# Top-k attention with an MLP behind it: scores in quarters of the PE array, and the left-over keys of the values in quarters too

## The chip, the core and the metric

The kernel runs on one core of a Trainium2 chip. The metric is the device time of one execution in microseconds, the median of several runs. Below, PE is TensorE (with its queue of stationary loads, PEld), DVE is VectorE, ACT is ScalarE, POOL is GpSimd and SP is SyncE, which issues the DMAs.

## The reference

Attention of 8 batches with 8 heads, 576 rows and 64 dimensions a head, in which each row keeps its 32 largest scores; behind it an MLP with a leaky ReLU over 4608 tokens of 512 features. All of it is in 32-bit floating point.

```python
scores = scale * np.matmul(q, k.transpose(0, 1, 3, 2))
kth = np.partition(scores, -32, axis=-1)[..., -32:-31]
scores = np.where(scores >= kth, scores, -1000000000.0)
attn = np.exp(scores - np.max(scores, axis=-1, keepdims=True))
attn = attn / (np.sum(attn, axis=-1, keepdims=True) + 1e-09)
x = np.matmul(attn, v)          # then (B, S, H*D), as 4608 x 512
h = x @ w_in                    # 512 x 2048
out = np.maximum(0.01 * h, h) @ w_out
```

## The kernel before, in words

**Units.** The 64 heads are held as 32 pairs, four pairs to a batch; a pair has the 64 dimensions of head 0 on partitions 0 to 63 and those of head 1 on 64 to 127. A unit is 128 rows of scores for each of two heads. 576 rows are four times 128 and 64 left over, so there are two sorts: a whole unit has 128 rows of one pair, and a grouped unit has the 64 left-over rows of two pairs, that is of four heads. A batch has 16 whole and 2 grouped units, 144 units in all. In batches 0, 2, ... the grouped units come last, in 1, 3, ... first (L202 to L206). Two neighbours in this order, here called a couple, always belong to the same sort, and for whole units to neighbouring pairs.

**Steps.** The loop at L609 has a step s for every unit. In a step DVE finds the top 32 of unit s (`top_k`, L289); POOL masks unit s-1 and ACT takes its exponents; unit s-2 is normalized by ACT, split into its 16-bit halves (L339), written to DRAM and read back transposed (L344), which gives `wT`, the weights by key. Work is issued in an order written out by hand, and each engine goes through its own queue in that order.

**Scores** (`scores`, L208) are made in even steps for a couple two units ahead. The 576 keys are cut into 352 and 224. A unit's 352 keys go to a PSUM tile "wide" of two banks (two such tiles rotate), and the 224 keys of both units share one tile "narrow". A head has its own bank (index i at L225). For a whole unit a matmul has 64 dimensions on one half of the rows of the array and 128 columns (rows of scores): two for each part, head 0 on the upper rows and head 1 on the lower. For a grouped unit a matmul has 64 rows and 64 columns, four for each part. ACT copies the results to `s_sb` (L232).

**Values** (`weigh_values`, L374; called by `values`, L593) are made for a couple as soon as its weights are there: in the middle of a step for units 0 to 13, at the end of a step afterwards (`values_at`, L495). Keys are taken in five chunks. Four are of 128 keys. The fifth holds the 64 left-over keys of both heads: the weights of head 0 on partitions 0 to 63, those of head 1 on 64 to 127 (`vk` has zeros in the half that belongs to the other head). A matmul has the 128 keys on the rows of the array and the 64 value dimensions on half of its columns; head 0 and head 1 take the two halves in turn. Each unit of a couple takes 10 matmuls with 128 columns moving; a grouped one takes 20 with 64 moving. All go to one bank of a "wide" tile, and ACT copies them to x (`keep_values`, L388, L395), where x tile number p holds the two heads of pair p on its 128 partitions.

**Order of the two.** Up to step 19 (`HURRY` = 20) the scores stand ahead of the values at the end of a step, afterwards the values stand ahead of the scores (L663 to L667). Three couples (`HURRIED`) have their values in an odd step, where no scores are made. For 12 units the scores are made at the start and kept in DRAM (`keep_scores`, `fetch_scores`), so six even steps make none.

**MLP** (`mlp`, L425). Chunks of 256 tokens (the first two 128) go through `w_in` (L437) and `w_out` (L449) in small portions between the attention work; `slot_budget` and `mlp_cost` decide from counts of columns how many portions stand in each slot. They know nothing of the cost of scores and values. What is left over at the end runs in one stretch. An f32 matmul shows in the trace as two records, each with its own stationary load.

Of the kernel before, what the change touches and what calls it, by code (L numbers as in the profile page):

```python
# [9 lines left out]
F32 = mybir.dt.float32  # L10
# [6 lines left out]
NKC = 5  # L17
# [3 lines left out]
def kernel(  # L21
# [13 lines left out]
    nc = tc.nc  # L35
    NPAIR, P, S = qT.shape
    D = P // 2
# [7 lines left out]
    HP = DMODEL // P  # L45
# [6 lines left out]
    LEFT = S % P  # L52
# [14 lines left out]
    ps_sc = ctx.enter_context(tc.tile_pool(name="ps_sc", bufs=1, space=bass.MemoryType.PSUM))  # L67
# [13 lines left out]
    w_in = [const.tile([P, DFF], F32, name=f"w_in{c}") for c in range(HP)]  # L81
# [78 lines left out]
    qk_of, v_of = {}, {}  # L160
# [20 lines left out]
    class Unit:  # L181
# [3 lines left out]
        def __init__(self, b, pairs, q0):  # L185
# [10 lines left out]
                self.outs = [(pairs[0], 0, LEFT), (pairs[1], LEFT, 0)]  # L196
            self.pairs = pairs

    units = []
    for b in range(B):  # L200
        first = b % 2 == 1
# [6 lines left out]
    def scores(us):  # L208


        narrow = ps_sc.tile([P, 2, 512], F32, name="narrow")
        ps = {}
        for k, u in enumerate(us):
            wide = ps_sc.tile([P, 2, 512], F32, name="wide", bufs=2)
            ps[u] = ((wide[:, :, 0:WIDE], 0, WIDE),
                     (narrow[:, :, k * NARROW:(k + 1) * NARROW], WIDE, S))

        order = ((us[0], 0), (us[0], 1), (us[1], 1), (us[1], 0))
        for u, part in order:
            to, k0, k1 = ps[u][part]  # L220
            for n in range(0, len(u.parts), 2):
                for i, pi, side, r0 in u.parts[n:n + 2]:
                    qt, kt = qk_of[pi]
                    d = slice(side * D, (side + 1) * D)
                    nc.tensor.matmul(to[r0:r0 + u.rows, i, :], qt[d, u.q0:u.q0 + u.rows],  # L225
                                     kt[d, k0:k1], start=True, stop=True)
        for u in us:
            u.both = work.tile([P, 2, S], F32, name="s_sb", bufs=5)
            u.s = [u.both[:, i, :] for i in range(2)]
        for u, part in order:  # L230
            to, k0, k1 = ps[u][part]
            nc.scalar.copy(u.both[:, :, k0:k1], to)  # L232
# [131 lines left out]
    x_of = {}  # L364

    def x_at(token):

        c = 0
        while token >= CHUNKS[c]:
            token -= CHUNKS[c]  # L370
            c += 1
        return c, token

    def weigh_values(u, po):  # L374
        n = u.rows
        po = po.rearrange("p (o n) -> p o n", n=n)
        for o, (pi, r0, r1) in enumerate(u.outs):
            vt = v_of[pi]
            for c in range(NKC):
                for side, r in ((0, r0), (1, r1)):  # L380
                    nc.tensor.matmul(  # L381
                        po[side * D:(side + 1) * D, o, :],
                        vt[:, c, side, :],
                        u.wT[:, c + side * NKC if c + 1 < NKC else c, r:r + n],
                        start=(c == 0), stop=(c == NKC - 1),
                    )

    def keep_values(u, po):  # L388
        n = u.rows
        po = po.rearrange("p (o n) -> p o n", n=n)  # L390
        ch, col = x_at(u.b * S + u.q0)
        if ch not in x_of:
            x_of[ch] = [xpool.tile([P, CHMAX], F32, name=f"x{c}") for c in range(HP)]
        for o, (pi, _, _) in enumerate(u.outs):
            nc.scalar.copy(x_of[ch][pi % HP][:, col:col + n], po[:, o, :])  # L395

    EARLY = 2

# [90 lines left out]
    HURRY = 20  # L489
# [3 lines left out]
    MIDDLE, END = 0, 1  # L493

    def values_at(n):  # L495

        if n < UNHURRIED:
            return (n | 1) + LAG + 1, MIDDLE
        return (n | 1) + LAG - ((n | 1) in HURRIED), END
# [10 lines left out]
    for n, u in enumerate(steps):  # L510
        ch, _ = x_at(u.b * S + u.q0)
# [5 lines left out]
    def attended(*place):  # L517
        for at, ch in ready_at:
            if at == place:
                ready.append(ch)  # L520
                backlog[0] += mlp_cost(ch)
# [12 lines left out]
    with tc.manual_schedule():  # L534
# [57 lines left out]

        def values(*place):  # L593
            due = [u for n, u in enumerate(steps) if values_at(n) == place]
            if due:
                po = ps_sc.tile([P, 2, 512], F32, name="wide", bufs=2)[:, 0, 0:2 * P]
                po = po.rearrange("p (u n) -> p u n", u=2)
            else:
                return ()
            for n, u in enumerate(due):  # L600
                weigh_values(u, po[:, n, :])
            return [(u, po[:, n, :]) for n, u in enumerate(due)]

        def keep(weighed, *place):
            for u, po in weighed:
                keep_values(u, po)
            attended(*place)

        for s in range(len(steps) + LAG + 1):  # L609
# [18 lines left out]
            if older and not late and not at_first:  # L628
                weights_of(older)
            mlp_steps(budget)  # L630
            weighed = values(s, MIDDLE)
            at_once = s - 2 in HASTY or any(at == (s, MIDDLE) for at, _ in ready_at)
            if at_once:
                keep(weighed, s, MIDDLE)
# [24 lines left out]
            if not at_once:  # L659
                keep(weighed, s, MIDDLE)  # L660
            if new and new[0] in early_units:
                new = ()
            if new and s < HURRY:  # L663
                scores(new)
            keep(values(s, END), s, END)
            if new and s >= HURRY:
                scores(new)  # L667
# [63 lines left out]
```

## Time and profile before

| what | us |
|---|---|
| median of 3 runs | 1464.25 (1464.2 to 1464.74) |
| the profiled execution | 1463.63 |
| its span, first to last instruction | 1461.7 |
| PE busy in it | 1405.5 |
| second layer of the MLP, L449, 1152 records of 128x512 | 505.1 |
| first layer of the MLP, L437, 2176 records of 128x256 | 482.6 |
| values, L381, 3200 records | 179.0 |
| scores, L225, wide tiles of whole units, 280 + 176 records of 64x352 | 60.1 + 35.0 |
| scores, L225, narrow tiles of whole units, 280 + 176 records of 64x224 | 34.9 + 21.3 |
| copies of values to x, L395, 160 | 32.2 |

Busy times of rows overlap where matmuls run beside each other. In a row of the profile, "128*64" is the part of the array that a record uses, rows by columns; "128x128" behind it is the moving operand, partitions by columns. The interval from one start to the next measures a stage better than the duration of a record, since the end of a matmul is modelled.

### The profile page before, as it was taken

To read this page: it belongs to the slowest core of one execution; us is meant where nothing else is said; L and a number is where in the kernel's file an instruction comes from. 1 tells how busy PE (TensorE), PEld (TensorE's weight loads), DVE (VectorE), ACT (ScalarE), POOL (GpSimd) and SP (SyncE) were. 2 spreads that over 40 slices of the span, in tenths; PEclk is the share of its full clock that TensorE was granted. 3 is DMA by queue.
4 is the path that set the end of the run, shared out by engine and by line. 5 is a ranking of instruction groups with operands and counts; after the bars stand their busy time and mean duration, and the time that the engine had idled before them with its cause. 6 is when DMAs were issued, how large, how long until landed. Compare 5 with 4: busy or idle time off the path is not lost.

```text
span 1461.7 us, 24213 instructions
## 1 busy us (share of the span) xinstructions
PE 1405.5 (96%) x8066; PEld 932.9 (64%) x8068; DVE 1320.3 (90%) x3401; ACT 1100.9 (75%) x1984; POOL 1097.8 (75%) x744
## 2 busy tenths in 40 slices
PE   7848999999989999999999999999999999999998
PEld 2425548576757676767676767676766666666674
DVE  7999999999999999999999999999999999999600
ACT  8878878677868777777778787777777777777710
POOL 3288888878888888888888787888887878787700
PEclk9968999999999999999999999999999999999999
DMA  8967543646576666676656655666566665554510
GB/s 320 344 219 225 140 119 101 194 128 181 151 192 179 172 167 188 156 194 169 157 163 170 169 138 141 171 164 166 149 156 171 164 151 143 153 141 130 150 43 14
DMA packets 394989, 239.03 MB, mean 164 GB/s; under 512 B 334576, under 2 KB 336112, under 8 KB 392944
## 3 DMA queue, kind: packets, MB, share of 16 engines
q1 hardware_dynamic: 394864, 237.48, 58.5%
q8 instruction: 63, 1.03, 0.3%
q14 instruction: 62, 0.51, 0.1%
HBM read 55.77 MB, written 99.09 MB: 106 GB/s over the span
## 4 chain that ended last, share of the span: by engine, by line
PE 77%; DVE 13%; ACT 4%; DMA 4%; issue 1%; SPq 0%; POOL 0%; DVEq 0%; ACTq 0%; POOLq 0%
PE pz L449 30%; PE ph L437 29%; PE wide L381 10%; DVE tops L301 5%; PE wide L225 5%; DVE pairs L304 4%; PE narrow L225 3%; DMA apart<-split 2%; ACT split L339 1%; DVE pairs L296 1%; DMA raw<-in_weights_dram 1%; ACT s_sb L318 1%; ACT s_sb L330 1%; DVE w_out L156 1%; DMA wT<-apart 1%
## 5 line engine op out<-in xcount | busy, mean ns | idle before, releaser
L314 POOL TENSOR_SCALAR pen<-s_sb,tops 128x576 f32<-128x576 f32 x288 | 638.3, 2216 | 203.8 <-DVE tops L301 135.6
L301 DVE MAX8 tops<-pairs 128x8 f32<-128x288 f32 (+1 forms) x1152 | 635.9, 591 | 0.0
L449 PE MATMUL pz<-w_out,gT 128*128 128x512 f32 x1152 | 505.1, 595 | 2.4 <-ACT scale L410 2.4
L437 PE MATMUL ph<-x,w_in 128*128 128x256 f32 x2176 | 482.6, 381 | 0.0
L304 DVE MATCH_REPLACE8 pairs<-tops,pairs 128x288 f32<-128x288 f32 (+1 forms) x864 | 460.1, 538 | 0.0
L437 PEld LDWEIGHTS ph<-x,w_in 128*128 128x128 f32 x2176 | 409.5, 190 | 75.5 <-issue 21.3
L315 POOL TENSOR_TENSOR s_sb<-s_sb,pen 128x576 f32<-128x576 f32 x288 | 406.9, 1413 | 24.0
L449 PEld LDWEIGHTS pz<-w_out,gT 128*128 128x128 f32 x1152 | 216.4, 190 | 266.2 <-issue 261.2
L339 ACT COPY split<-s_sb 128x1152 uint16<-128x1152 uint16 x280 | 309.5, 1146 | 1.7 <-DMA apart<-split 1.7
L330 ACT ACTIVATE s_sb<-s_sb,rz 128x576 f32<-128x576 f32 x288 | 207.7, 773 | 33.4 <-DVE rz L327 33.4
L318 ACT ACTIVATE s_sb<-s_sb,nbias 128x576 f32<-128x576 f32 x288 | 222.4, 772 | 6.4 <-POOL s_sb L315 6.4
L296 DVE TENSOR_TENSOR pairs<-s_sb 128x576 f32<-128x576 f32 x288 | 213.6, 780 | 9.5
L381 PEld LDWEIGHTS wide<-wT,vt 128*64 128x64 f32 x3200 | 161.2, 139 | 53.0 <-issue 36.2
L381 PE MATMUL wide<-wT,vt 128*64 128x128 f32 (+1 forms) x3200 | 179.0, 268 | 10.3 <-DMA wT<-apart 4.7
L443 ACT ACTIVATE gT<-ph 128x512 f32<-128x512 f32 x136 | 80.7, 593 | 58.6 <-PE ph L437 57.7
L395 ACT COPY x<-wide 128x128 f32<-128x128 f32 (+1 forms) x160 | 32.2, 260 | 120.2 <-PE wide L381 120.2
L232 ACT COPY s_sb<-wide 128x704 f32<-128x704 f32 x130 | 98.0, 754 | 20.1 <-PE wide L225 20.1
L458 ACT COPY o_sb<-pz 128x512 f32<-128x512 f32 x36 | 21.1, 585 | 92.3 <-PE pz L449 92.2
L225 PE MATMUL wide<-kt,qt 64*128 64x352 f32 (+1 forms) x360 | 70.4, 507 | 1.0 <-ACT s_sb L247 0.7
L232 ACT COPY s_sb<-narrow 128x448 f32<-128x448 f32 x130 | 62.9, 536 | 1.2 <-PE narrow L225 0.6
L304 DVE MATCH_VALUE_LOAD pairs<-tops,pairs 128x8 f32 x864 | 62.6, 72 | 0.0
L327 DVE RECIPROCAL rz<-ze 128x2 f32<-128x2 f32 x144 | 22.3, 155 | 42.3 <-ACT ze L323 42.1
(67 smaller groups left out, 678.0 us busy)
## 6 DMA issues: line engine op xcount, KB each, us to landing
apart<-split SPq DMA_DIRECT2D x280, 288.0 KB, 2.1
raw<-in_weights_dram SPq DMA_DIRECT2D x15, 1024.0 KB, 6.9
vt<-in_vk_dram SPq DMA_DIRECT2D x32, 320.0 KB, 3.7
out_dram<-o_sb SPq DMA_DIRECT2D x36, 256.0 KB, 2.8
kept<-gT SPq DMA_DIRECT2D x12, 576.0 KB, 3.2
s_sb<-kept SPq DMA_DIRECT2D x12, 576.0 KB, 4.8
qt<-in_qT_dram SPq DMA_DIRECT2D x20, 288.0 KB, 3.5
kt<-in_kT_dram SPq DMA_DIRECT2D x20, 288.0 KB, 3.4
```

What stands on the lines that cost most here:

```text
L225: nc.tensor.matmul(to[r0:r0 + u.rows, i, :], qt[d, u.q0:u.q0 + u.rows], kt[d, k0:k1], start=True, stop=True)
L296: nc.vector.tensor_tensor(pairs[:, :, n, :], u.both[:, :, 0:HS], u.both[:, :, HS:S], op)
L301: nc.vector.max(out=u.tops[:, i, r, :], in_=rest[i])
L304: nc.vector.match_replace(out=rest[i], in_to_replace=u.tops[:, i, r, :], in_values=rest[i], imm_value=LOWEST)
L314: nc.gpsimd.tensor_scalar(pen, u.s[i], u.tops[:, i, ROUNDS - 1, 7:8], MASKED, ALU.is_lt, ALU.mult)
L315: nc.gpsimd.tensor_tensor(u.s[i], u.s[i], pen, ALU.add)
L318: nc.scalar.activation(u.s[i], u.s[i], AF.Exp, bias=u.nbias[:, i:i + 1], scale=SCALE, accum_out=u.z[:, i:i + 1])
L330: nc.scalar.activation(u.s[i], u.s[i], AF.Copy, bias=0.0, scale=u.rz[:, i:i + 1])
L339: nc.scalar.copy(split, pairs[:, :, h])
L381: nc.tensor.matmul(po[side * D:(side + 1) * D, o, :], vt[:, c, side, :], u.wT[:, c + side * NKC if c + 1 < NKC else c, r:r + n], start=(c ...
L437: nc.tensor.matmul(ph[:, i, 0:n], w_in[c][:, f * P:(f + 1) * P], x[c][:, 0:n], start=(c == 0), stop=(c == HP - 1),)
L449: nc.tensor.matmul(pz[0:m, 0:DMODEL], gT[:, f, r0:r0 + m], w_out[f // 4][:, f % 4, :], start=(f == 0), stop=(f == NFC - 1),)
```

## The change

**Scores.** A whole unit's matmuls are cut into rows 0 to 63 and 64 to 127: four of 64 x 64 for each part where there were two of 64 x 128. A grouped unit's are the same as before, in the same order.

**Values of whole units** (`weigh_whole`). A couple is done together. The two halves of columns now belong to the two units, the two banks of the "wide" tile to the two heads. Four chunks of keys are as before but for the order. The fifth is taken in 64-row pieces: only the head's own 64 keys, so that the four matmuls of a chunk (two heads by two units) lie on the four quarters of the array. These stand last where the scores follow (from step 20), first otherwise; for units 0 to 13 the fifth chunk stays 128 rows with its zeros.

**Values of grouped units** (`weigh_left`) take the same matmuls with halves of columns by pair and banks by head.

**x** now has head 0 of two neighbouring pairs in one tile, head 1 in the next; the host puts the rows of `w_in` in the same order.

```diff
+            self.quarters = [(i, pi, side, r0 + r, q0 + r) for r in range(0, self.rows, LEFT)
+                             for i, pi, side, r0 in self.parts]
...
-            for n in range(0, len(u.parts), 2):
-                for i, pi, side, r0 in u.parts[n:n + 2]:
+            for n in range(0, len(u.quarters), 4):
+                for i, pi, side, r0, q0 in u.quarters[n:n + 4]:
                     qt, kt = qk_of[pi]
                     d = slice(side * D, (side + 1) * D)
-                    nc.tensor.matmul(to[r0:r0 + u.rows, i, :], qt[d, u.q0:u.q0 + u.rows],
+                    nc.tensor.matmul(to[r0:r0 + LEFT, i, :], qt[d, q0:q0 + LEFT],
                                      kt[d, k0:k1], start=True, stop=True)
...
-    def weigh_values(u, po):
...
+    def weigh_whole(us, po, order):
+        for m, c in enumerate(order):
+            for side in range(2):
+                k = slice(side * LEFT, (side + 1) * LEFT) if c == QUARTERS else slice(0, P)
+                at = min(c, NKC - 1)
+                for n, u in enumerate(us):
                     nc.tensor.matmul(
+                        po[n * D:(n + 1) * D, side, 0:P],
+                        v_of[u.pairs[0]][k, at, side, :],
+                        u.wT[k, at + side * NKC if at + 1 < NKC else at, :],
+                        start=(m == 0), stop=(m == NKC - 1),
+                    )
+
+    def weigh_left(u, po):
+        for c in range(NKC):
+            for side in range(2):
+                for o, (pi, *rows) in enumerate(u.outs):
+                    r = rows[side]
+                    nc.tensor.matmul(
+                        po[o * D:(o + 1) * D, side, :],
+                        v_of[pi][:, c, side, :],
+                        u.wT[:, c + side * NKC if c + 1 < NKC else c, r:r + LEFT],
                         start=(c == 0), stop=(c == NKC - 1),
                     )
...
+    def keep_values(pair, po, b, q0):
+        ch, col = x_at(b * S + q0)
...
+        for side in range(2):
+            nc.scalar.copy(x_of[ch][pair % HP + side][:, col:col + po.shape[-1]], po[:, side, :])
+
+    QUARTERS = NKC
+    FULL = list(range(NKC - 1))
...
+            po = ps_sc.tile([P, 2, 512], F32, name="wide", bufs=2)
+            if len(due[0].pairs) == 1:
+                weigh_whole(due, po, FULL + [NKC - 1] if place[1] == MIDDLE else
+                            [QUARTERS] + FULL if place[0] < HURRY else FULL + [QUARTERS])
+                return [(due[0], po[:, :, 0:P])]
             for n, u in enumerate(due):
+                weigh_left(u, po[:, :, n * LEFT:(n + 1) * LEFT])
+            return [(u, po[:, :, n * LEFT:(n + 1) * LEFT]) for n, u in enumerate(due)]
...
+        w_in = w_in.reshape(2, 2, 2, 64, 2048).transpose(0, 2, 1, 3, 4)
```

## The prediction, made before the change was run

> **What bounds the kernel now.** I read the page first: busy shares, the slices, and the engines of the chain of work that ended last.
>
> ```profile
> PE 1405.5 (96%) x8066; PEld 932.9 (64%) x8068; DVE 1320.3 (90%) x3401; ACT 1100.9 (75%) x1984; POOL 1097.8 (75%) x744
> PE   7848999999989999999999999999999999999998
> DVE  7999999999999999999999999999999999999600
> PE 77%; DVE 13%; ACT 4%; DMA 4%; issue 1%; SPq 0%; POOL 0%; DVEq 0%; ACTq 0%; POOLq 0%
> ```
>
> PE is full in nearly every slice and makes 77% of the chain; but DVE is nearly full too, so I asked for the busy time by stretch, and for what PE waited for from 250 us on.
>
> ```profile
> 431.00:650.00 219.00, 218.39 (x1336) 149.81 (x1338) 215.09 (x561) 168.70 (x315) 183.11 (x122) 0.99 0.66 176
> 650.00:943.00 293.00, 292.67 (x1736) 199.80 (x1732) 281.90 (x732) 232.46 (x426) 238.71 (x160) 1.00 0.60 161
> ```
>
> ```profile
> PE wide L381 <- DMA wT<-apart: 4.7, 2, 4.2
> PE wide L381 <- DMA vt<-in_vk_dram: 2.0, 2, 1.7
> ```
>
> The columns of the first are length, then PE, PEld, DVE, ACT and POOL busy. From 431 us to the end PE has no gap worth naming; DVE is idle 3.9 of 219 us, later 11.1 of 293 us. So a microsecond taken from PE's stream is a microsecond of time, as long as DVE keeps up. The 4.2 us wait lies at 427 us: there the chain had run over DVE from 381 us.
>
> What one even step costs PE I took from the timeline of PE. First a couple of whole units (two units of 128 rows and two heads), then a later one whose scores belong to units of four heads:
>
> ```profile
> 701.77 2.40 PE L381 MATMUL wide<-wT,vt 128*64 128x128 f32 x40
> 704.10 0.86 PE L225 MATMUL wide<-kt,qt 64*128 64x352 f32 x4
> 704.80 0.92 PE L225 MATMUL narrow<-kt,qt 64*128 64x224 f32 x8
> 705.55 0.76 PE L225 MATMUL wide<-kt,qt 64*128 64x352 f32 x4
> 706.24 1.13 PE L437 MATMUL ph<-x,w_in 128*128 128x256 f32 x4
> ...
> 522.16 2.40 PE L381 MATMUL wide<-wT,vt 128*64 128x128 f32 x40
> 524.49 0.82 PE L225 MATMUL wide<-kt,qt 64*64 64x352 f32 x8
> 525.14 0.94 PE L225 MATMUL narrow<-kt,qt 64*64 64x224 f32 x16
> 525.89 0.77 PE L225 MATMUL wide<-kt,qt 64*64 64x352 f32 x8
> 526.60 0.70 PE L437 MATMUL ph<-x,w_in 128*128 128x256 f32 x2
> ```
>
> Read starts, not durations: matmuls overlap. An f32 matmul is two records (two passes). From start to next start the values take 2.33 us, the scores 2.14 us, and the scores in 64*64 pieces, twice as many, 2.10 us. Narrower windows show the seams:
>
> ```profile
> 703.89 0.28 PE L381 MATMUL wide<-wT,vt 128*64 128x128 f32 x2
> 704.10 0.57 PE L225 MATMUL wide<-kt,qt 64*128 64x352 f32 x2
> 704.50 0.46 PE L225 MATMUL wide<-kt,qt 64*128 64x352 f32 x2
> ```
>
> ```profile
> 524.49 0.53 PE L225 MATMUL wide<-kt,qt 64*64 64x352 f32 x4
> 524.84 0.48 PE L225 MATMUL wide<-kt,qt 64*64 64x352 f32 x4
> ```
>
> Two records of the values start together (7 ns apart in the trace), one such pair each 109 ns. The last pair starts at 703.893, the scores at 704.103 rather than 109 ns later: 0.10 us of standstill at the change of tile shape. The first pass of the scores then takes 0.40 us, the others 0.296: another 0.10 us, the first stationary load, which nothing hides. With 64 columns (524.49 to 524.84) the first pass takes 0.347, so that exposed load is 0.05 us. And four records of 64*64 start within 20 ns of each other: the four quarters do run at once.
>
> **The Trainium skill.** "TensorEngine Tiling (Array Packing)", Key Properties: a change of tiling mode drains TensorE, and different tiles work in parallel. The trace agrees: 0.10 us at the seam, quads 7 ns apart. "TensorE: Matmul & The Clock Gate", LDWEIGHTS: the load's time goes with its columns, not its rows. The trace agrees: 0.10 us exposed for 128 columns, 0.05 for 64. "TensorEngine Tiling (Array Packing)", Gotcha 1: different row tiles may not write one PSUM bank at once; that is why the change puts the heads of a unit in two banks. No run shows the opposite.
>
> **The change part by part**, for an even step in which a couple's values are followed by scores. Before: 2.334 + 2.141 = 4.475 us (medians of the trace).
>
> *Full keys.* Four of five chunks stay as 128*64 pairs, in another order (side outside, unit inside, so the two columns of tiles are two units rather than two heads). 40 records become 32, 16 pairs instead of 20. First to last start was 2.132; less four pairs of 109 ns: 1.695. To the next stage another 0.203 as now, the drain within it: 1.898.
>
> *Left-over keys.* 8 records instead of 8, but four at a time: two passes. The first has the exposed 64-column load: 109 + 51 = 160. The second 109 if streaming sets it. The trace before has no quad with 128 columns moving; the nearest rows are the quads of 224 (190 ns a pass, as the pairs) and the pairs of 64 moving columns in the grouped values, 58 ns for two loads and two matmuls, so four of each in at most 117. I take 113: together 0.273.
>
> *Scores.* Sixteen quads in place of sixteen pairs' worth of the same streaming; 2.101 by the grouped row, less the 51 ns of first load, since the mode is already 64*64 and the loads can run under the last quarter: 2.050. Those 16 further matmuls with loads per couple are hidden under the streaming, as the grouped row shows.
>
> Sum 1.898 + 0.273 + 2.050 = 4.221: 0.254 us less. With grouped scores behind (before 2.101) 0.214 less. With no scores behind the values: 1.898 + 0.160 + 0.113 + 0.094 of drain = 2.265 against 2.334: 0.069 less. Whole scores after grouped values, or alone: 0.040 less. The grouped units' own values keep their 80 records and their scores their order: nothing. Units 0 to 13 (values in the middle of a step) keep the zero-padded fifth chunk: nothing.
>
> *Copies.* Two ACT copies of 128x128 before and after, 0.27 us each. Both of before already began after the couple's last matmul (0.32 and 0.48 us after its start), so nothing is late by taking heads instead of units. ACT stands waiting for them (1.2 to 2.1 us idle ahead of each couple in mid-kernel), which covers them. The scores need the copied buffer again only at their last part, 1.35 us in. The rearranged rows of w_in cost nothing on the chip; loads, DMAs and the queues of SP and POOL are as they were.
>
> *How often, and where it counts.* Counting stages in the trace: from 650 us on 30 couples with whole scores behind, 4 with grouped scores, 3 with none, 4 grouped values with whole scores: 30 x 0.254 + 4 x 0.214 + 3 x 0.069 + 4 x 0.040 = 8.85. From 431 to 650: 5, 2, 3, 2: 1.99. From 287 to 379 us, where the chain is PE's before it goes over to DVE: 3 and 3: 0.97. Between, and before 287, DVE, ACT or DMA end last and PE's gain is idle time. Sum 11.8 us.
>
> *Does DVE keep up?* Its steady step is 8.84 us (the same line starts in the chain at 387.31 and, three steps on, at 413.84), 17.7 a couple; PE's couple is 18.53 in the later batches (701.84 to 868.63 in nine), 18.27 after. From 431 to 650 PE's couple is 18.1, and DVE's idle there, 3.9 us, covers 1.99. At 380.5 us DVE had waited 0.92 us, about the 0.97 that would come earlier. I take off 0.5 us for these two tight places: 11.3 us.
>
> The profiled execution is 1463.63 us, its span 1461.7 and 1.9 around it; the gain gives 1452.3 there. The median is 1464.25: 1453.0.
>
> **Rivals.**
> *DVE takes over.* For: DVE 98% busy from 431 to 650. Then the 1.99 and the 0.97 are lost, and a little later too when a light couple (17.6 us at 739.51 to 757.14) falls below that: gain 8 to 9, 1455.5. Against: later batches have 0.8 us of slack a couple.
> *The quarters go two at a time* (two row tiles with the same columns accumulating). Then four passes, 160 + 3 x 109 = 0.487; a couple with scores gains 0.04, one without loses 0.145. In all under 1 us: 1463.5. Against: the pairs of the scores before are two row tiles, the pairs of values two column tiles, the grouped scores both.
> *Slower: the quarters of the values go one after the other*, being accumulation in banks that 128*64 tiles have just written. Eight records of 109 and the first load, 0.923 instead of 0.273: a couple with scores loses 0.396, with none 0.58; from 287 us on 38 x 0.40 + 6 x 0.44 + 9 x 0.58 = 23, less the little that the lone scores gain: about 1487. It decides from 0.527 us for the eight records (238 ns a pass). For it only that no quad which accumulates is in the trace.
> *The change doesn't do what it says*: if scores still drain behind the quarters, each couple gives back 0.15: 11.8 - 43 x 0.15 leaves 5: 1459. Against: both are 64-row, 64-column tiles.
>
> **How the numbers follow.** Forecast 0.72 (own range 1451 to 1455), DVE 0.13, scores that drain 0.05, two at a time 0.05, serial 0.05. The range holds the first two with the unknown pass (109 to 117 ns: 0.4 us either way) and half a microsecond for places before 431 us that may gain more: 1450.5 to 1458. A measurement of this kernel tells 0.2%, 2.9 us, from no change: faster 0.90, same 0.05, slower 0.05.
>
> **What would show it.** Right: values 128*64 in 32 records and 8 of 64*64 behind them, four within some 20 ns, two passes about 0.16 and 0.11 us; the first pass of the scores at 0.296 rather than 0.40, with no gap ahead; values and scores together 4.22 us; PE still full from 431 us. Wrong: gaps of PE in the values or scores with a DVE or transposed-weights wait behind them; quad starts 100 ns apart; scores that begin 0.2 us after the last quarter.

## The result, and the profile after

The changed kernel took 1460.55 us (median of 20 runs, 1457.87 to 1465.11) against 1464.6 us for the kernel before measured beside it: a ratio of 0.9975, 95% interval [0.9968, 0.9982]. Measured again with the experiments, it was 1464.07 us against 1464.44: 0.9999 [0.9991, 1.0007]. So it gained between nothing and 4 us, where 11.3 were forecast. The profiled execution is 1460.92 us, its span 1458.9.

The page of the changed kernel first: busy shares, and the engines of the chain of work that ended last.

```profile
PE 1397.0 (96%) x8978; PEld 904.6 (62%) x8980; DVE 1319.8 (90%) x3401; ACT 1101.0 (75%) x1984; POOL 1096.4 (75%) x744
PE 74%; DVE 12%; DMA 7%; ACT 5%; issue 1%; SPq 0%; POOL 0%; DVEq 0%; ACTq 0%; POOLq 0%
```

PE's busy time fell by 8.5 us and its share of the chain from 77 to 74%. DVE did not take that share, it fell too; DMA rose from 4 to 7%. Busy time by stretch (length, then PE, PEld, DVE, ACT, POOL) and PE's waits from 250 us on say where:

```profile
431.00:650.00 219.00, 214.75 (x1420) 144.74 (x1421) 212.23 (x554) 168.66 (x312) 179.71 (x121) 0.98 0.67 174
650.00:943.00 293.00, 293.00 (x2002) 195.31 (x2001) 284.51 (x740) 233.97 (x431) 240.78 (x161) 1.00 0.62 164
```

```profile
PE wide L386 <- DMA wT<-apart: 10.9, 6, 6.1
PE wide L398 <- DMA vt<-in_vk_dram: 2.1, 1, 2.1
```

Before, PE missed 0.6 of the first 219 us; now it misses 4.3. Most of that is one wait, which ended at 431.61 us before and now ends at 434.85, so that this stretch takes in more of it. With both edges 5 us later PE misses 0.4 us:

```profile
436.00:655.00 219.00, 218.60 (x1482) 147.00 (x1482) 212.23 (x556) 168.77 (x313) 180.15 (x121) 1.00 0.67 174
```

So PE is as full as before once that wait is over. What has grown is the waits on the transposed weights: 4.7 us in 2 places before, 10.9 in 6 now. The couple itself is as forecast. The timeline of PE, a couple with whole scores behind:

```profile
705.10 2.35 PE L386 MATMUL wide<-wT,vt 128*64 128x128 f32 x40
707.27 0.77 PE L228 MATMUL wide<-kt,qt 64*64 64x352 f32 x8
707.86 0.94 PE L228 MATMUL narrow<-kt,qt 64*64 64x224 f32 x16
708.62 0.77 PE L228 MATMUL wide<-kt,qt 64*64 64x352 f32 x8
709.32 0.48 PE L455 MATMUL ph<-x,w_in 128*128 128x256 f32 x1
```

705.10 to 709.32 is 4.22 us, where it was 4.47. The 40 records are 32 in halves and 8 in quarters (the line names the first form only). A narrow window on the seam of another couple shows the 8, and the first scores behind them:

```profile
671.41 0.45 PE L386 MATMUL wide<-wT,vt 64*64 64x128 f32 x8
671.68 0.48 PE L228 MATMUL wide<-kt,qt 64*64 64x352 f32 x4
```

The eight take 0.27 us, and the scores begin with no drain.

What the forecast had not seen stands in the timeline wherever the second unit's weights land late. The first place, before (three lines of it), and then the changed kernel:

```profile
285.91 1.31 PE L381 MATMUL wide<-wT,vt 128*64 128x128 f32 x20
287.67 1.31 PE L381 MATMUL wide<-wT,vt 128*64 128x128 f32 x20 [0.44 <-DMA wT<-apart]
288.91 0.86 PE L225 MATMUL wide<-raw 64*128 64x352 f32 x4
```

```profile
283.60 0.43 PE L386 MATMUL wide<-wT,vt 128*64 128x128 f32 x2
286.07 3.04 PE L386 MATMUL wide<-wT,vt 128*64 128x128 f32 x38 [2.04 <-DMA wT<-apart]
288.89 1.40 PE L228 MATMUL wide<-raw 64*64 64x352 f32 x8
```

The number to read is the count. Before, 20 records, all of the first unit, were done when PE met the missing weights, and 20 were left. In the changed kernel it is 2 and 38: the units take turns matmul by matmul, so the second one's weights are wanted from the start, and 0.43 us into the couple PE stands still (1.31 us before). The changed kernel came to this place 2.31 us early and left it 0.02 us early. At 428 us it is worse:

```profile
426.05 1.31 PE L381 MATMUL wide<-wT,vt 128*64 128x128 f32 x20
431.61 2.40 PE L381 MATMUL wide<-wT,vt 128*64 128x128 f32 x20 [4.25 <-DMA wT<-apart]
433.94 1.27 PE L225 MATMUL wide<-kt,qt 64*128 64x352 f32 x4
```

```profile
428.34 0.43 PE L386 MATMUL wide<-wT,vt 128*64 128x128 f32 x2
434.85 3.67 PE L386 MATMUL wide<-wT,vt 128*64 128x128 f32 x38 [6.08 <-DMA wT<-apart]
438.35 0.77 PE L228 MATMUL wide<-kt,qt 64*64 64x352 f32 x8
```

Here it leaves 4.4 us late, and it takes until 961 us to make that up at some 0.25 us a couple. At 249 us, ahead of the first of these places, this execution was 2.76 us early, and it ends 2.7 us early: over the whole rest the cheaper couples gave no more than the late weights took.

To put a number on it for a whole run I took every stage of values from 230 us on in the trace, from its first record to the next stage, and summed what it took over the fastest of its kind. Before, this excess is 6.9 us, in the changed kernel 18.5. All values and scores from 230 us on take 279.4 us before and after: 12.7 us of cheaper stages, eaten by 11.5 us of excess in the values, 0.6 in the scores and 0.5 in one stage that is alone of its kind.

### The profile page after: what moved, and what is told of

Same layout as the page of the kernel before. It is cut to its first block, busy times and chain, and to the rows that moved or that the text cites. A ratio compares the mean times of both kernels' runs of the same rounds, so it can differ in the third digit from the quotient of the medians.

```text
span 1458.9 us, 26037 instructions
## 1 busy us (share of the span) xinstructions
PE 1397.0 (96%) x8978; PEld 904.6 (62%) x8980; DVE 1319.8 (90%) x3401; ACT 1101.0 (75%) x1984; POOL 1096.4 (75%) x744
## 4 chain that ended last, share of the span: by engine, by line
PE 74%; DVE 12%; DMA 7%; ACT 5%; issue 1%; SPq 0%; POOL 0%; DVEq 0%; ACTq 0%; POOLq 0%
PE ph L455 28%; PE pz L467 28%; PE wide L386 9%; DVE tops L304 5%; PE wide L228 4%; DVE pairs L307 4%; DMA apart<-split 3%; PE narrow L228 3%; DMA wT<-apart 3%; ACT split L342 2%; DVE pairs L299 1%; PE wide L398 1%; ACT s_sb L321 1%; ACT s_sb L333 1%; DMA raw<-in_weights_dram 1%
## 5 line engine op out<-in xcount | busy, mean ns | idle before, releaser
L386 PE MATMUL wide<-wT,vt 128*64 128x128 f32 (+1 forms) x2560 | 160.3, 284 | 14.5 <-DMA wT<-apart 10.9
L386 PEld LDWEIGHTS wide<-wT,vt 128*64 128x64 f32 (+1 forms) x2560 | 132.4, 139 | 63.8 <-issue 41.3
L228 PE MATMUL wide<-kt,qt 64*64 64x352 f32 x640 | 66.3, 476 | 1.0 <-ACT s_sb L250 0.7
```

The lines of the kernel that those rows point to most:

```text
L228: nc.tensor.matmul(to[r0:r0 + LEFT, i, :], qt[d, q0:q0 + LEFT], kt[d, k0:k1], start=True, stop=True)
L386: nc.tensor.matmul(po[n * D:(n + 1) * D, side, 0:P], v_of[u.pairs[0]][k, at, side, :], u.wT[k, at + side * NKC if at + 1 < NKC else at, :] ...
```

## The experiments

Two theories. *Both weights*: the order of the values asks for the transposed weights of both units at once and so uncovers the second one's DMA. *DVE caps*: the couples are cheaper, but DVE and what hangs on it set the pace up to 650 us, whatever the order. The first four kernels below ran on one chip, beside 1464.44 us for the kernel before (25 runs), the last four on another, beside 1465.13 us (41 runs); across the two I compare ratios. That is rough to some 0.2%: the changed kernel's own ratio was 0.9975 in the first set of runs and 0.9999 in the second.

### e0: the changed kernel again

> The changed kernel as it is, for comparison on the same chip. Both theories: about 1460.5 us, 4 us under the kernel before.

Measured 1464.07 us (13 runs, 1461.86 to 1467.75), 0.9999 [0.9991, 1.0007], 3.5 us over what both theories expected. The excess of its values is 20.5 us. The changed kernel scatters: 24 of its stages of values exceed the fastest by over 0.05 us, against four before. PE waits for transposed weights in nine places.

### e1: scores in quarters alone

```diff
+            self.quarters = [(i, pi, side, r0 + r, q0 + r) for r in range(0, self.rows, LEFT)
+                             for i, pi, side, r0 in self.parts]
...
-            for n in range(0, len(u.parts), 2):
-                for i, pi, side, r0 in u.parts[n:n + 2]:
+            for n in range(0, len(u.quarters), 4):
+                for i, pi, side, r0, q0 in u.quarters[n:n + 4]:
...
-                    nc.tensor.matmul(to[r0:r0 + u.rows, i, :], qt[d, u.q0:u.q0 + u.rows],
+                    nc.tensor.matmul(to[r0:r0 + LEFT, i, :], qt[d, q0:q0 + LEFT],
```

> The kernel before with the scores of whole units in quarters, values as before. Theory 'both weights' (in the changed kernel a couple's values can begin only when the transposed weights of both units have landed, so the first unit's 1.2 us no longer run under the second one's DMA): nothing of that is in here, so some 44 couples with scores gain 0.04 us each: 1.7 us under the kernel before. Theory 'DVE caps' (the couples got cheaper as forecast, but DVE and the DMA chain behind it set the pace up to 650 us): the gain before 650 us is lost, about 1.3 us under it.

Measured 1464.09 us: 0.9993 [0.9984, 1.0002]. The interval holds no change and both theories: inconclusive. In its trace the scores stage takes 2.10 us instead of 2.14, as forecast. Its profiled execution was its slowest (1468.12 us): it shows that late weights can cost this order too (excess 12.7).

### e2: units in turn, without quarters in the values

```diff
-                weigh_whole(due, po, FULL + [NKC - 1] if place[1] == MIDDLE else
-                            [QUARTERS] + FULL if place[0] < HURRY else FULL + [QUARTERS])
+                weigh_whole(due, po, FULL + [NKC - 1])
```

> The changed kernel with all five chunks of the values on 128 rows, so that the order of the two units in turn, the scores in quarters and the two banks stay, but no left-over keys in quarters. 'Both weights': the waits of the changed kernel stay and the gain of the quarters is gone: 5 to 7 us over e1, that is slower than before by 3 to 6 us, with PE waits on the transposed weights of over 8 us from 300 us on. 'DVE caps': the order of units costs nothing: as e1 within 1 us.

Measured 1473.13 us: 1.0064 [1.005, 1.0077]. This kernel has the same 40 records of one shape a couple as the one before, only in turn, and is 9.0 us slower than e1, which differs from it in that order (with banks and halves to match); 5 to 7 us were expected. Its waits:

```profile
PE wide L386 <- DMA wT<-apart: 12.7, 11, 6.8
PE wide L398 <- DMA vt<-in_vk_dram: 2.0, 1, 2.0
```

Eleven waits rather than the two before, and an excess of 21.3 us; the trace of e1, its slowest execution, has four (9.7 us). *DVE caps* expected e1 within 1 us, and falls: the order costs time.

### e3: unit by unit, with the quarters

For the first unit head 0 takes columns 0 to 63 and head 1 the others; for the second they are swapped. So each unit fills both halves by itself, and the four quarters of both still fit on the array at the end.

```diff
-        for m, c in enumerate(order):
+        def chunk(n, u, m, side):
...
+            col = n ^ side
+            nc.tensor.matmul(
+                po[col * D:(col + 1) * D, side, 0:P],
...
-                for n, u in enumerate(us):
-                    nc.tensor.matmul(
-                        po[n * D:(n + 1) * D, side, 0:P],
...
+        for n, u in enumerate(us):
+            for m in whole:
+                for col in range(2):
+                    chunk(n, u, m, n ^ col)
+        if order[-1] == QUARTERS:
+            quarters(NKC - 1)
...
-                        po[o * D:(o + 1) * D, side, :],
+                        po[(o ^ side) * D:((o ^ side) + 1) * D, side, :],
...
+        w_in[:, 1] = w_in[:, 1, ::-1].copy()
```

> The changed kernel with the four full chunks unit by unit (head 0 and head 1 on the two halves of columns, swapped for the second unit, w_in's rows to match) and the four quarters of both units at the end. The work on PE is the same to the record. 'Both weights': the first unit's 0.87 us of full chunks run again under the second one's DMA, and the time falls to 1453 to 1456 us. 'DVE caps': 1460 us as the changed kernel.

Measured 1455.4 us (1452.57 to 1456.12): 0.9936 [0.9924, 0.9948], 8.7 us under the changed kernel with the same records on PE. The first place again, in this kernel:

```profile
284.84 1.10 PE L383 MATMUL wide<-wT,vt 128*64 128x128 f32 x16
286.18 1.47 PE L383 MATMUL wide<-wT,vt 128*64 128x128 f32 x24 [0.24 <-DMA wT<-apart]
287.47 0.77 PE L228 MATMUL wide<-raw 64*64 64x352 f32 x8
```

The weights land 0.1 us later than in the changed kernel (286.18 against 286.07), but 16 records are done by then, PE stood for 0.24 us and not 2.04, and the stage ends 1.4 us earlier. Excess of the values 12.3 us.

### e7: the layout of e3, chunk by chunk

```diff
-        for n, u in enumerate(us):
-            for m in whole:
+        for m in whole:
+            for n, u in enumerate(us):
                 for col in range(2):
```

> The layout of e3 (heads on the two halves of columns, swapped for the second unit), but chunk by chunk with the two units in turn, as the changed kernel does. 'Both weights': it is the order, not the layout: as the changed kernel, 1460 to 1464 us. If the layout helped: as e3, 1455 us.

Measured 1462.36 us (21 runs, 1458.28 to 1464.99): 0.998 [0.9973, 0.9986]; excess 21.3 us in the trace, which is of its slowest execution. Two loops change places against e3, nothing else, and 0.44% come back, 6.4 us. Where the weights are there in time a couple's values take 2.166 us in e3, in e7 and in the changed kernel: on PE itself the order costs nothing, only the waits differ. e3 ran on the other chip; on this one e5 and e6 below, which are unit by unit and in turn, are 5.5 us apart. It is the order, not the layout.

### e4: unit by unit, scores in halves

The scores of e3 are put back as in the kernel before.

```diff
-            for n in range(0, len(u.quarters), 4):
+            for n in range(0, len(u.parts), 2):
...
-                    nc.tensor.matmul(to[r0:r0 + LEFT, i, :], qt[d, q0:q0 + LEFT],
+                    nc.tensor.matmul(to[r0:r0 + u.rows, i, :], qt[d, u.q0:u.q0 + u.rows],
```

> Unit by unit as e3, but the scores of whole units in 64 x 128 pieces as before. If the seams cost what the forecast took (0.10 us of drain and 0.05 us of exposed load more for each of some 44 couples), 5 to 6 us over e3: about 1461 us. If the quarters of the values alone bring the gain, as e3 within 1.5 us.

Measured 1462.92 us: 0.9985 [0.9978, 0.9991], 0.49% or 7.2 us over e3. In its trace the values end 0.11 us later than in e3 (the drain is back) and the scores take 2.14 us instead of 2.05: 0.20 a couple, 7.6 us for 38 couples. So without scores of the same shape behind them the quarters leave about 2 us of gain, and most of the gain hangs on the scores behind them having the same shape. I had written 0.15: the exposed load is then the one of 128 columns, 0.10 and not 0.05 us.

### e5 and e6: one more unit transposed on PE

```diff
-    HASTY = (14, 15, 23, 31)
+    HASTY = (14, 15, 23, 31, 37)
```

e6 is the changed kernel with it:

> The changed kernel with unit 37 transposed by PE. 'Both weights': its largest wait, 5.5 to 6.1 us, goes, for 1.4 us of transposes: 2 to 4 us under the changed kernel on the same chip. 'DVE caps': no gain.

e5 is e3 with it:

> As e3, with unit 37 transposed by PE and not by DMA (one more entry in HASTY). If the transposed weights' DMA ends the wait of 6 us at 425 us, that wait goes and PE pays some 1.4 us of transposes: 2 to 4 us under e3, 1451 to 1453. If DVE's pace ends it in truth, no gain: 1455 to 1457.

Measured 1456.36 us (0.9943 [0.9929, 0.9957]) for e6, and 1450.88 us (1450.38 to 1451.06; 0.9903 [0.989, 0.9917]) for e5: the fastest of all, 14.2 us under the kernel before on that chip. By the ratios this is more than the 2 to 4 us expected of either. The timeline of PE in e5, where e3 waits 5.96 us:

```profile
416.00 1.43 PE L357 MATMUL wide<-ident,s_sb 128*128 128x128 f32 x9
417.27 8.75 PE L479 MATMUL pz<-w_out,gT 128*128 128x512 f32 x20
425.95 2.35 PE L383 MATMUL wide<-wT,vt 128*64 128x128 f32 x40
428.12 0.77 PE L228 MATMUL wide<-kt,qt 64*64 64x352 f32 x8
```

Nine transposes, 1.3 us of PE, and the couple runs through without a gap. All its waits on transposed weights together:

```profile
PE wide L383 <- DMA wT<-apart: 2.1, 4, 1.1
```

Its excess is 3.5 us, below the 6.9 of the kernel before.

So the two DMAs, the write of the split weights and the transposed read, belong to what ended the wait at 425 us. DVE isn't cleared by that. In e3 the chain of work that leads to this wait runs over DVE from 380 to 420 us, and only then over SP and the DMAs (start, length, what; the last DVE piece, and the DMAs):

```profile
419.64 0.68 DVE tops L304
421.57 5.68 DMA apart<-split
427.30 4.65 DMA wT<-apart
```

And in e5, with the wait gone, the chain runs over DVE from 402 to 459 us, and PE waits 1.9 us for ACT between 430 and 461 us.

## Why the prediction was wrong

The forecast was 1453.0 us in a range of 1450.5 to 1458; the changed kernel came out at 1460.55.

*What held.* The price of the couple. Values with scores behind them were to take 2.171 us and take 2.166 (fastest stage of the trace), with none behind 2.265 and take 2.276; the scores 2.050, measured 2.049; together 4.221, measured 4.215. The quads run at once, the first of the two passes takes 0.16 and the second 0.11 us, and the drain between quarters and scores is gone. The sum over all couples, 11.8 us forecast, is 12.7 in the trace, which counts from 230 us on. Copies and loads cost nothing that these stages show. That DVE keeps up held for most of the time: with the waits out of the way e5 reaches 1450.88 us, though DVE and ACT set its pace from 402 to 461 us; from 465 us on its PE waits only for transposed weights, 1.4 us in two places.

*The step that failed* stands under "Full keys": "Four of five chunks stay as 128*64 pairs, in another order (side outside, unit inside, so the two columns of tiles are two units rather than two heads)". I priced the order at nothing, because the records are the same. It decides when the second unit's weights must be there. Before, the first unit's 1.17 us (half of 2.33) ran under the second one's DMA; with the unit inside, only the first unit's first matmul does, two of the couple's 40 records. The profile of before had this in view: the 4.25 us wait at 427 us stood between 20 records and 20, between the two units. I read it as the place where DVE had the chain, and didn't ask what PE had done ahead of it. For the copies I had asked when their inputs are there and what they wait for; for the loads of the values I had not. The sign that the forecast had named for being wrong came: gaps of PE in the values with a transposed-weights wait behind them.

What it cost: e7 against e3 and e2 against e1, which change the order each in another surrounding, give 6.4 and 9 us; the changed kernel lost 7.2 us against the forecast in the first set of runs, 11 in the second. That is more than one unit's cover in six places (0.88 us each, 1.31 less 0.43), since a late couple can make later weights late: at 284, 396 and 428 us in turn the changed kernel fell from 2.3 us ahead to 4.4 behind. How the couple at 396 us reaches the one at 428 its chain of work shows (start, length, what):

```profile
397.37 2.34 PE wide L386 x38
401.64 10.57 PE ph L455 x48
412.73 2.20 ACT split L342 x2
414.95 5.78 DMA apart<-split
424.78 5.45 DMA apart<-split
430.27 4.53 DMA wT<-apart
```

The first layer of the MLP stands behind the couple and ends late, ACT waits for it ahead of the split of the first unit's weights, and SP takes up the second unit's write only after the first one's transposed read, 1.7 us after its split was done (422.6 us, write at 424.3). These weights land 3.2 us later than before. In e0 the chain to the same wait runs over DVE instead, so this path isn't the only one.

*The rival "DVE takes over"* pointed at the right stretch, 287 to 650 us, but isn't what the changed kernel lost by: e2 against e1 and e7 against e3 leave DVE its work and change the order alone, and the time goes with the order. There is some truth in it for what is left in e3. There the weights of unit 37 hang on DVE and the two DMAs behind it: PE arrives 1.11 us earlier than before, the weights do not, the wait at 425 us grows from 4.25 to 5.96 us, and e3 leaves 0.44 us late. That accounts for most of the 2.4 us by which e3 missed 1453. Going round the DMAs, as e5 and e6 do, gains 0.33% (4.8 us) over e3 and 0.32 to 0.56% over the changed kernel (4.7 us by its first ratio, 8.2 by its second). The rivals with two quarters at a time and with quarters in a row are excluded by the seam above; scores that still drain are what e4 shows.

What stays open: how much of the changed kernel's loss is direct cover and how much the delay handed on isn't separated. Nor was it tried why its two measurements differ by 4 us; that its waits hang on when a DMA lands fits, but isn't shown to be the reason.

## What to carry to other kernels

When two streams of work are interleaved so that an array is shared between them, the interleaved block starts when the later input is there: cost the order by the arrival of its operands, not by its count of instructions. If both streams can be laid out so that each fills the array alone, take them one after the other and interleave only the part that needs both. And put stages of one tile shape side by side: here the quarters gained 0.15% with another shape behind them (e4) and 0.64% with the same one (e3, where the scores are in quarters too).

## What had not been expected of the hardware

Late weights can cost twice, since TensorE's granted clock can fall after the wait. Busy time by stretch of the changed kernel, where the third figure from the end is the granted clock:

```profile
280.00:286.00 6.00, 4.03 (x11) 1.52 (x9) 5.97 (x15) 3.18 (x5) 4.83 (x4) 1.00 0.60 159
286.00:290.20 4.20, 4.13 (x50) 3.12 (x54) 4.20 (x14) 0.43 (x2) 3.99 (x3) 0.67 0.48 169
```

A wait of 2.04 us was followed by 0.67 of the clock on average, half of it from 287.4 to 290.8 us: the 38 records took 2.8 us to the next stage (2.15 in the couple at 396 us, which stopped after two records too), and the scores 0.97 us more than the fastest. "TensorE: Matmul & The Clock Gate" in the Trainium skill (Part 1) gives about 3.4 us of idleness for this. Here some 2 us were enough, but not always: at 193 us PE has a gap of 2.14 us in the kernel before and in the changed one alike. The clock behind it was 0.66 in the one and 1.00 in the other, the next scores 3.29 us and 2.10. That made 1.8 us of the changed kernel's lead there (1.1 us at 180 us, 2.8 at 202).

What differs is where the gap lies. In all ten traces the granted clock is either full or half, and from 70 us on each change of it lies on a grid of 3.41 us. In the kernel before one slot of this grid holds 2.0 us of the gap, and the next slot has half the clock; in the changed kernel an edge cuts the gap in two, the longer part is 1.4 us, and the clock stays. Two slots of each kernel, the one before first (the second figure is PE's busy time):

```profile
192.46:195.87 3.41, 1.40 (x4) 0.68 (x4) 3.38 (x8) 3.41 (x7) 2.21 (x4) 1.00 0.44 99
195.88:199.28 3.40, 3.40 (x26) 1.40 (x28) 3.40 (x10) 2.83 (x6) 3.22 (x3) 0.50 0.45 174
```

```profile
191.86:195.26 3.40, 2.00 (x8) 0.77 (x12) 3.37 (x6) 3.40 (x7) 2.28 (x3) 1.00 0.30 72
195.28:198.68 3.40, 3.40 (x36) 1.69 (x36) 3.40 (x12) 3.37 (x9) 3.22 (x3) 1.00 0.41 156
```

From 180 us on, in all ten traces, a slot at full clock in which PE idled for up to 1.86 us was followed by the full clock, and one in which it idled for 2.00 us or more by half. Before 180 us the border is less sharp: half the clock came after 1.34 us in one slot, the full one after 1.99 in another. The edges lie at other places in each execution, so which gap is hit is luck, and this part of the lead has nothing to do with the change.
